# Gelu's table loaded by a one-column activation, small sine tables made after the first normalized tiles, table arguments kept in w2's tile, and a new order of work

## The chip, the cores and the metric

The kernel runs on one core of a Trainium2 chip. A core has a matrix engine (TensorE, PE in the profile; its weight loads are shown as PEld), a vector engine (VectorE, DVE), an activation engine (ScalarE, ACT), GpSimd (POOL), and SyncE (SP), which here only issues DMAs. Each engine works through its own instructions strictly in the order in which they were written and waits on semaphores for the others. The metric is the device time of one execution in microseconds (us), compared by the median over runs.

## The reference

`x` is `A_q` (2048 x 640, bf16). It is layer-normalized to `xn`, which feeds two branches:

```python
xn = _layernorm(x, axis=-1)
# A: four-tap causal shift convolution of k, times v, then a causal convolution over 2048 places
k_shift = sum over t of k_pad[:, t:t + S, :] * shift_k[:, ks - 1 - t]
kv = k_shift * v
y = irfft(rfft(kv padded to 2 S) * rfft(ssm_k padded))[:S] + kv * ssm_D
s = xn * y
# B: a two-layer MLP, 640 -> 1728 -> 640
g = silu(gelu(xn @ w1 + b1) @ w2 + b2)
return x + s * g
```

Here `gelu` is the tanh approximation.

## The kernel before, in words

Sequence rows are held as 16 tiles of 128 partitions x 640 columns. The kernel is a list of small named operations, each tied to one engine, and a string `ORDER` that names them in the order in which they are written out. This order is fixed by hand; each engine's queue is the sub-list of its own operations. `/A` and `/D` behind a name put an eviction from PSUM on ACT or on DVE. Where two operations share a buffer the framework adds the semaphore wait. Temporary buffers come from pools, handed out first-freed-first in the order of the string: three PSUM pairs `ps`, two PSUM banks `psf`, four staging buffers `st`, three gate buffers `sl`.

The names that matter:

- Loads on SP: `xl` (x), `Kl` (the long filter ssm_k, held for now in x and xn tiles 8 to 15; `Kl4` is the small piece with filter tiles 6 and 7), `w1l`, `w2l`, `kl` (k), `vl` (v). `b1l`, `skl` (the shift taps) and `Dl` are issued by ACT.
- Sine tables. `wq`, `wr` on DVE compute integer arguments (L223 to L229) in a scratch `Pq`, and `ws0`, `ws1`, `ws2` on ACT (L234) turn them into the first Fourier matrix W with Sin. The small tables F2 and I1 come from `sm0` (seven iotas on POOL, L242 to L247), `sm1` (nine small DVE instructions), `ss` (two Sin activations on ACT, L271 and L272) and `sx` (a scaling on POOL, L275).
- `warm` and `dm0`, `dm1`, `dm2`: matmuls on zeros, whose results nobody reads (L666, L673). `wm`/`we`: the shift taps broadcast to all partitions (PE L321, evicted by L176).
- Layer norm by tile: `bn` (DVE L382, L383), `rs` (POOL L395, L396), `xn` (DVE L401), `xt` (PE transposes L411), `xe` (eviction L176).
- MLP: `f1` (PE L431; `f1h`, L445, the last 64 columns of w1), `ge`/`geh` (Gelu, ACT L437, L451), `f2` (PE L467), `si` (Silu, ACT L471), `gx` (xn times gate, DVE L473). A name such as `f1_1_0_9` is: chunk of four tiles, part, column tile of w1. Column tiles 0-1, 2-4, 5-8 and 9-13 of w1 arrive with `w1l0` to `w1l3`.
- Convolution: `kv` (taps and product with v, DVE L495 to L504), stage 1 `K1`, `K1r` for the filter and `U1`, `U1r` for kv (PE L342, L357), evicted by `Ke`, `Ker`, `Ue`, `Uer` (L176) and written to scratch DRAM by `Ks`, `Us` (SP). They are read back transposed by `KL`, `UL`; stage 2 `K2`, `U2`, `X2` (PE L538, L552); products `pm`, `pq` (DVE L567); stage 3 `j1`, `j1r` (PE L573); `cs` and `cl` go through scratch DRAM once more; the last stage is `i2` (PE L640), then `ym` (times xn, DVE L644), `ad` (plus x, DVE L648, L656) and `os` (store). `Da` (POOL L303) adds ssm_D to the filter's first row.

The activation tables are loaded by an instruction that the compiler puts ahead of the first activation of a new set. If that activation waits for a matmul, so does the load.

Of the kernel before, what the change touches and what calls it, by code (L numbers as in the profile page):

```python
# [99 lines left out]
def h3_block(ctx: ExitStack, tc: tile.TileContext, x_d, k_d, v_d, sk_d, K_d, D_d, w1_d, b1_d, w2_d, out_d):  # L100
# [139 lines left out]
    def sm0(e):  # L240
        g = nc.gpsimd
        g.iota(pi, pattern=[[0, 1]], base=0, channel_multiplier=1)  # L242
        g.iota(k2s, pattern=[[0, 1]], base=0, channel_multiplier=1, allow_small_or_imprecise_dtypes=True)
# [1 line left out]
        g.iota(ng, pattern=[[0, 6], [1, 16], [16, 2]], base=0, channel_multiplier=0, allow_small_or_imprecise_dtypes=True)
# [446 lines left out]
ge_0_1_3 K1_10 K1_1 ge_0_1_2 ge_1_0_10 Ke_10/A f1_0_0_10 ge_0_0_10 f1_0_1_4 ge_0_0_11 ge_0_1_4 ge_0_1_5 Ke_1/A
f1_0_1_6 f1_0_2_12 ge_0_1_6 kv1_1a Da ge_0_1_7 K1r_0 rs4 vl1 w2l1 ge_0_2_12 K1_0 w2l0 xn15 f1_0_1_0 Ke_2/A ge_0_1_0
ge_0_1_1 f1_0_1_10 ge_0_1_11 kl2 ge_0_1_10 f1_0_0_8 kv1_2m kv1_2a ge_0_0_9 ge_0_0_8 f1_0_1_8 Ke_0/A ge_0_1_8 Ks_5
ge_0_1_9 xn12 kv1_3m kv1_3a Ker_0/A Ks_4 kv1_4 kv2_0 vl2 f2_7_1 kv2_1m Ks_0 kv2_1a kv2_2m si_7_1 gx_7_1 Ks_1 kv2_2a
kl3 kv2_3m ss f2_3_1 U1_2 Ue_2/A si_3_1 U1_3 U1r_0 Uer_0/A Ue_3/A f2_1_1 si_1_1 U1_1 gx_1_1 Us_1 f2_0_1 Ue_1/A kv2_3a
gx_3_1 kv2_4 kv3_1m kv3_0 si_0_1 vl3 U1_0 Ue_0/A Us_0 U1_7 U1r_1 Uer_1/A f2_6_0 U1_4 Ue_7/A U1_6 Ue_6/A si_6_0 f2_5_0
gx_0_1 kv3_1a gx_6_0 Ue_4/A kv3_2m kv3_2a si_5_0 gx_5_0 kv3_3m kv3_3a xn14 U1_8 U1_9 U1_5 kv3_4 f2_4_1 Us_3 Ue_5/A
Ue_9/A xt12 si_4_1 U1r_2 U1_10 kv4_0 gx_4_1 Ue_8/A xe12/A xl4 kv4_1m f2_5_1 KL1 f2_6_1 Uer_2/A U1_11 si_5_1 gx_5_1
kv4_1a kv4_2m bn8 KL2 kv4_2a Ue_10/A si_6_1 Ue_11/A U1_12 Us_4 U1_13 xt14 xe14/A Us_2 Ue_12/A Ue_13/A f2_2_1 kv4_3m  # L700
# [1 line left out]
xt15 Uer_3/A Ue_14/A f2_3_0 xe15/A K2_1 Ue_15/A Us_6 si_3_0 xn13 f2_0_0 Kf_1_0/A si_0_0 f2_4_0 si_4_0 Us_7 sx gx_3_0
KL0 rs3 xn9 gx_0_0 xn10 xt9 K2_3 xe9/D Kf_1_1/A xt10 f2_7_0 xn11 xn8 Kf_3_0/D xe10/A Kf_3_1/A xt13 si_7_0 K2_0 f2_1_0
gx_7_0 xe13/A Kf_0_1/A Kf_0_0/D gx_4_0 UL0 UL1 UL3 si_1_0 xt11 xe11/A X2_0 Xf_0/D U2_0 xt8 xe8/D gx_1_0 Uf_0_1/A
pq_0_0 f1_3_0_1 UL2 ge_3_0_1 UL5 Uf_0_0/D pq_0_1 UL4 U2_1 Uf_1_1/A f1_3_0_0 ge_3_0_0 Uf_1_0/D pm_1_0 pm_1_1 f1_2_0_4
ge_2_0_4 U2_3 X2_1 Uf_3_0/A Uf_3_1/A f1_2_0_7 ge_2_0_7 f1_3_0_11 pm_0_1 j1_1 Xf_1/A je_1_1/A f1_3_0_5 ge_3_0_11
je_1_0/D ge_3_0_5 X2_3 pm_0_0 U2_2 f1_2_0_11 Uf_2_1/A Uf_2_0/D gt f1_3_0_9 Xf_3/A j1_0 ge_2_0_11 f1_2_0_1 ge_3_0_9
je_0_1/A pq_1_0 pq_1_1 j1r_0 ge_2_0_1 pm_2_1 jer_0_1/A je_0_0/D KL4 UL7 jer_0_0/A f1_2_0_0 pm_2_0 X2_2 ge_2_0_0 K2_4
f1_3_0_4 Xf_2/D Kf_4_1/A pm_3_0 Kf_4_0/A ge_3_0_4 j1_2 f1_2_0_5 je_2_1/A je_2_0/D X2_4 U2_4 ge_2_0_5 f1_3_0_8 pm_3_1
f1h_2 KL5 Uf_4_0/D Xf_4/A j1_3 Uf_4_1/A cs_0 ge_3_0_8 geh_2 pq_2_1 pq_2_0 f1_2_0_10 je_3_0/A K2_5 pq_3_0 pm_4_1 cs_1  # L710
je_3_1/D ge_2_0_10 UL6 f1_2_0_6 Kf_5_1/A U2_6 KL6 Kf_5_0/D X2_5 pq_4_0 f1_3_0_7 Uf_6_0/D ge_2_0_6 Uf_6_1/A U2_5 Xf_5/A
Uf_5_0/A f1_3_0_10 pq_3_1 pm_4_0 j1_4 Uf_5_1/D ge_3_0_7 ge_3_0_10 pq_5_0 X2_6 f1_3_0_2 je_4_0/A je_4_1/D j1r_1 Xf_6/A
jer_1_1/A ge_3_0_2 KL7 pm_5_1 pm_5_0 jer_1_0/A f1_3_0_6 K2_7 Kf_7_1/A Kf_7_0/D f1_2_0_3 X2_7 pq_6_1 ge_3_0_6 Xf_7/D
cs_2 K2_6 Kf_6_0/A f1_2_0_12 j1_5 pq_5_1 pq_7_0 pq_6_0 Kf_6_1/D ge_2_0_3 ge_2_0_12 f1_2_0_2 je_5_0/A U2_7 ge_2_0_2
Uf_7_0/A cs_3 f1_3_0_12 f1_3_0_3 Uf_7_1/A ge_3_0_12 pq_7_1 pq_4_1 je_5_1/D pm_6_0 j1r_2 pm_6_1 f1_2_0_8 ge_3_0_3
jer_2_0/A ge_2_0_8 jer_2_1/D j1r_3 f1_2_0_9 jer_3_1/A j1_6 ge_2_0_9 cs_5 pm_7_0 f2_11_0 jer_3_0/D cs_4 pm_7_1 je_6_1/A
# [47 lines left out]
```

## Time and profile before

| | |
|---|---|
| median of 3 runs | 185.07 us (185.06 to 185.65) |
| profiled execution | 184.39 us, span 182.60 us |
| PE busy | 175.6 us, 96% of the span |
| DVE busy | 157.8 us, 86% |
| ACT busy | 143.9 us, 79% |
| POOL busy | 16.4 us, 9% |
| DMA | 50.32 MB, mean 276 GB/s |

The span runs from the first to the last instruction; the profiled execution's own time is 1.79 us longer. Busy times are the union of an engine's instructions. In a timeline row the columns are start, duration, engine, source line, operation, tiles and shapes, and in brackets the idle time before it with what ended it. Rows of neighbours that are alike are merged.

### The profile page before, as it was taken

How to read it: one execution, taken by the hardware profiler on the slowest of the kernel's cores; microseconds unless marked ns; L12 is line 12 of the kernel's file. 1: busy time of each engine (PE TensorE's matmuls, PEld its weight loads, DVE VectorE, ACT ScalarE, POOL GpSimd, SP SyncE). 2: the span in 40 equal slices, each digit the busy share in tenths (PEclk: the TensorE clock that was granted, in tenths of full speed). 3: DMA queues.
4: the chain of work that ended last, by engine and by line, in shares of the span. 5: the costliest groups of instructions: out<-in, count | busy, mean ns of one | idle time of the engine just before them, and what ended most of it. 6: DMA issues, size and time to landing. Idle time of an engine off the chain costs nothing.

```text
...
## 1 busy us (share of the span) xinstructions
PE 175.6 (96%) x2109; PEld 104.0 (57%) x2109; DVE 157.8 (86%) x258; ACT 143.9 (79%) x212; POOL 16.4 (9%) x32
## 2 busy tenths in 40 slices
...
GB/s 152 353 396 314 274 380 375 301 419 403 404 52 356 335 340 372 359 306 284 289 391 310 90 224 385 242 166 147 163 127 108 317 157 344 304 250 323 117 216 180
DMA packets 24503, 50.32 MB, mean 276 GB/s; under 512 B 3807, under 2 KB 18465, under 8 KB 24226
## 3 DMA queue, kind: packets, MB, share of 16 engines
...
HBM read 31.14 MB, written 18.35 MB: 271 GB/s over the span
## 4 chain that ended last, share of the span: by engine, by line
PE 72%; DVE 11%; ACT 11%; DMA 2%; issue 2%; SPq 0%; ACTq 0%
PE psf L431 27%; PE psf L467 25%; DVE xn L644 6%; PE ps L573 6%; PE ps L538 5%; ACT st L176 4%; PE ps L342 4%; ACT hT L437 3%; DVE x L648 3%; DMA x<-in_ssm_k 2%; PE psf L411 2%; DVE xn L473 1%; PE ps L552 1%; DVE x L656 1%; ACT ku L176 1%
## 5 line engine op out<-in xcount | busy, mean ns | idle before, releaser
L467 PE MATMUL psf<-w,hT 128*64 128x320 bf16 (+6 forms) x672 | 65.0, 299 | 0.0
L431 PE MATMUL psf<-xnT,w 128*128 128x512 bf16 (+1 forms) x320 | 61.9, 340 | 0.1
L467 PEld LDWEIGHTS <-hT 128*64 128x64 bf16 (+3 forms) x672 | 47.5, 106 | 14.8 <-issue 3.2
L431 PEld LDWEIGHTS <-w 128*128 128x128 bf16 x320 | 28.9, 98 | 27.8 <-issue 9.2
L176 ACT CAST ku<-ps 128x1024 bf16<-128x1024 f32 (+1 forms) x42 | 39.3, 961 | 2.4 <-PE ps L321 0.8
L176 ACT CAST st<-ps 128x1024 bf16<-128x1024 f32 x39 | 39.3, 1028 | 0.3 <-PE ps L342 0.2
L437 ACT ACTIVATE hT<-psf,b1f 128x512 bf16<-128x512 f32 (+1 forms) x64 | 36.9, 619 | 2.9 <-PE psf L431 2.5
L471 ACT ACTIVATE sl<-psf 128x320 bf16<-128x320 f32 (+2 forms) x32 | 14.3, 445 | 26.8 <-PE psf L467 21.2
L176 DVE CAST ku<-ps 128x1024 bf16<-128x1024 f32 (+1 forms) x25 | 28.7, 1153 | 4.8 <-PE ps L573 2.6
L567 DVE TENSOR_TENSOR st<-ku 128x512 bf16<-128x512 bf16 (+1 forms) x32 | 25.0, 815 | 0.6 <-PE ps L573 0.5
L473 DVE TENSOR_TENSOR xn<-xn,sl 128x320 bf16<-128x320 bf16 (+2 forms) x32 | 10.1, 322 | 11.7 <-ACT sl L471 11.7
L499 DVE TENSOR_TENSOR ku<-ku 128x2560 bf16<-128x2560 bf16 (+1 forms) x15 | 19.1, 1275 | 0.2
L502 DVE TENSOR_TENSOR ku<-ku 128x2560 bf16<-128x2560 bf16 (+1 forms) x15 | 18.2, 1214 | 0.2
L382 DVE BATCH_NORM_STATS2 stats<-x 128x6 f32<-128x320 bf16 x32 | 13.7, 469 | 0.2 <-DMA x<-in_x 0.2
L644 DVE TENSOR_TENSOR xn<-ps,xn 128x640 bf16<-128x640 f32 x16 | 12.5, 814 | 1.4 <-PE ps L640 1.4
L573 PE MATMUL ps<-st,I 32*64 32x512 bf16 (+1 forms) x384 | 11.2, 344 | 0.0
L538 PE MATMUL ps<-ku,F 64*32 64x512 bf16 x256 | 10.0, 380 | 0.0
L176 ACT COPY xnT<-psf 128x640 bf16<-128x640 bf16 x12 | 8.4, 724 | 0.0
L573 PEld LDWEIGHTS <-I 32*64 32x64 bf16 x384 | 4.8, 104 | 6.1 <-issue 3.8
L411 PE MATMUL psf<-ident,xn 128*128 128x128 bf16 x80 | 7.0, 220 | 1.0 <-ACT hT L437 0.7
L401 DVE TENSOR_SCALAR xn<-x,mv,rstd 128x640 bf16<-128x640 bf16 x16 | 7.5, 492 | 0.1
L411 PEld LDWEIGHTS <-xn 128*128 128x128 bf16 x80 | 5.1, 97 | 4.2 <-issue 2.8
...
## 6 DMA issues: line engine op xcount, KB each, us to landing
...
```

The costliest lines, as they stand in the source:

```text
L176: (nc.scalar.copy if e == "ACT" else nc.vector.tensor_copy)(out=out_, in_=in_)
L411: nc.tensor.transpose(out=o[:, t, :], in_=xn_t[:, i, t * P:(t + 1) * P], identity=ident[:])
L431: nc.tensor.matmul(out=pb.v[:, u * n:u * n + n], lhsT=w1_t[:, ft, t, :], rhs=xnTb[c].v[:, a // P:(a + n) // P, t, :], start=(t == 0), stop ...
L437: op("ge_%d_%d_%d" % (c, r, ft), "ACT", lambda e, c=c, ft=ft, u=u, a=a, n=n, pb=pb: nc.scalar.activation(out=hTb[c].v[:, ft, a:a + n], in_ ...
L467: nc.tensor.matmul(out=pb.v[m:n, 0:hw], lhsT=hTb[c].v[0:M, ft, q * P + m:q * P + n], rhs=w2_t[0:M, ft, hs], start=(ft == 0), stop=(ft == F ...
L471: op("si_%d_%d" % (i, h), "ACT", lambda e, pb=pb, s_=s_, hw=hw: nc.scalar.activation(out=s_.v[:, 0:hw], in_=pb.v[:, 0:hw], func=ACT.Silu), ...
L499: op("kv%d_%dm" % (r, j), "DVE", lambda e, i=i, n=n, j=j, t=t, wb=wb: nc.vector.tensor_tensor(out=t.v[:, 0:n, :], in0=k_t[:, i + 3 - j:i + ...
L502: op("kv%d_%da" % (r, j), "DVE", lambda e, n=n, t=t, a=a: nc.vector.tensor_tensor(out=a.v[:, 0:n, :], in0=a.v[:, 0:n, :], in1=t.v[:, 0:n, ...
L538: nc.tensor.matmul(out=pb[ri].v[32 * j:32 * j + 32, a, :], lhsT=F2_t[64 * a:64 * a + 64, ri, :], rhs=B.v[64 * a:64 * a + 64, j, 0:512], st ...
L567: nc.vector.tensor_tensor(out=o, in0=u, in1=k, op=ALU.mult)
L573: nc.tensor.matmul(out=pb[j // 2].v[64 * a:64 * a + 64, j % 2, 0:n], lhsT=I1_t[32 * j:32 * j + 32, t, :], rhs=rhs(slice(32 * j, 32 * j + 3 ...
L644: op("ym_%d" % i, "DVE", lambda e, i=i, pb=pb: nc.vector.tensor_tensor(out=xn_t[:, i, :], in0=pb.v.rearrange("p a b -> p (a b)")[:, 0:D], ...
```

## The change

Four edits:

1. A new operation `tg`: one Gelu activation of one column, from the constant `cst` into a new tile `tg` that nothing reads. It stands on ACT behind `ws0` and ahead of the first `ge`, and waits only for the constant, so the load of Gelu's table stands ahead of it and not ahead of the first `ge`.
2. `sm0` now reads the first two normalized tiles: it begins with a POOL copy of two elements of them, so its seven iotas come after `xn0` and `xn1`.
3. The scratch `Pq` lies in w2's tile and not in k's. So the load of w2's first piece waits for the `ws`, and the first two loads of k no longer do.
4. `IDLE` has 10, 2 and 4 matmuls in place of 10, 6 and 5, and `ORDER` is new. `Kl4` is issued ahead of `xl0` and `xl1`, `w1l2` ahead of `xl3`, `w1l3` ahead of `Kl2`, and both ahead of the first `Ks`; `xn1` is made ahead of `xn0`; `f1_1_0_9` is the second matmul group of its chunk (it was the eighth); `KL2` is ahead of `KL1`; `ss` is later; the last stage takes its tiles in another order. From `xt9` to `f2_10_0` the order on PE is the same.

```diff
+    tg = sb.tile([P, 1], F32, name="tg")
...
-    Pq = k_t.rearrange("p a d -> p (a d)")[:, 0:4096].bitcast(I32)
+    Pq = w2_t[:].rearrange("p a d -> p (a d)")[:, 0:4096].bitcast(I32)
...
     def sm0(e):
         g = nc.gpsimd
+        g.tensor_copy(out=sct[0:1, 88:90], in_=xn_t[0:1, 0:2, 0])
         g.iota(pi, pattern=[[0, 1]], base=0, channel_multiplier=1)
...
-    op("sm0", "POOL", sm0, writes=[smb])
...
+    op("tg", "ACT", lambda e: nc.scalar.activation(out=tg[:], in_=cst[:, 0:1], func=ACT.Gelu_apprx_tanh), reads=[cb])
...
-             writes=[kb[g]] + (Pqb if g < 2 else []))
+             writes=[kb[g]])
...
+    op("sm0", "POOL", sm0, reads=[xnb[0][0], xnb[1][0]], writes=[smb])
...
-        load("w2l%d" % g, "SP", [(w2_t[:, a:b, :], w2_d[:, a:b, :])] + rest, writes=[w2b[g]])
+        load("w2l%d" % g, "SP", [(w2_t[:, a:b, :], w2_d[:, a:b, :])] + rest, writes=[w2b[g]] + (Pqb if g == 0 else []))
...
-IDLE = ((10, 1), (6, 1), (5, 0))
+IDLE = ((10, 1), (2, 1), (4, 0))
 ORDER = """
-xl0 b1l grid xl1 zz warm skl Kl4 one0 id Dl fix c0 wq1 wq2 wr1 ws1 wr2 xl3 xl2 w1l0 bn0 ws2 K1_6 one1 b1c bn1 rs0 sm0
-wm2 wm0 dm0 wq0 we0/A w1l2 w1l1 wr0 Ke_6/A wm1 dm1 xn0 we1/A xt0 xn1 bn6 bn4 Kl1 xe0/A bn5 xt1 dm2 xe1/A bn7 f1_0_0_6
-we2/D ws0 rs2 f1_0_0_4 K1_7 Kl3 ge_0_0_6 ge_0_0_7 bn3 Ke_7/D bn2 kl0 ge_0_0_4 K1r_1 ge_0_0_5 xn4 K1_5 Ker_1/A f1_0_0_0
-f1_0_0_2 Ke_5/A ge_0_0_1 ge_0_0_0 xn7 ge_0_0_3 ge_0_0_2 xn5 K1_14 K1_4 Ks_3 Kl2 xt4 xt7 Ke_4/A w1l3 K1_12 xe4/D rs1
-xe7/A xn6 xn2 xt5 xe5/D kv0_1m kv0_0 xn3 kv0_1a kv0_2m sm1 Ke_12/A xt6 Ks_2 K1r_3 xt2 xl5 K1_15 xe6/A xe2/A kv0_2a
-bn12 bn14 f1_1_0_6 Ke_15/A ge_1_0_6 f1_1_0_1 ge_1_0_1 Ker_3/A f1_1_0_8 ge_1_0_8 f1_1_0_0 ge_1_0_0 K1_11 Ke_14/A f1h_1
...
+zz grid c0 Kl4 b1l Dl warm one0 id one1 fix wq1 xl0 wq2 wr1 wr2 skl xl1 bn0 bn1 b1c rs0 ws1 w1l2 K1_6 wm0 xl3 ws2 wq0
+we0/A wr0 xn1 xn0 bn6 Ke_6/A bn5 bn7 wm2 dm0 bn4 wm1 dm1 we1/A xt1 w1l0 xe1/A xt0 xl2 w1l1 Kl1 K1_7 dm2 xe0/A f1_0_0_6
+f1_0_0_4 ws0 tg ge_0_0_7 ge_0_0_6 we2/D ge_0_0_4 ge_0_0_5 sm0 K1_5 rs2 Ke_5/A K1r_1 Ker_1/A f1_0_0_0 f1_0_0_2 ge_0_0_1
+ge_0_0_0 bn2 bn3 rs1 Ke_7/D Kl3 ge_0_0_3 ge_0_0_2 kl0 xn4 xn7 xn5 K1_4 Ke_4/A K1_15 K1_12 xt4 xe4/D xt7 xe7/A xn6 xt5
+xn2 Ke_12/A xe5/D xt6 K1r_3 xt2 kv0_0 K1_14 w1l3 Kl2 xe6/A f1_1_0_0 xe2/A kv0_1m Ke_15/A f1_1_0_9 ge_1_0_0 ge_1_0_9
+Ker_3/A sm1 kv0_1a Ks_3 f1_1_0_6 f1_1_0_8 K1_8 xl5 Ks_2 ge_1_0_6 ge_1_0_8 f1h_1 f1_1_0_11 xn3 geh_1 kv0_2m Ke_14/A
+bn14 kv0_2a kv0_3m bn12 ge_1_0_11 Kl0 vl0 bn13 Ks_7 f1_1_0_1 ge_1_0_1 xt3 K1_13 kl1 K1_11 xe3/A f1_1_0_4 Ke_13/A Ks_6
...
-kv4_3a kv4_4 si_2_1 K2_2 KL3 gx_6_1 Us_5 bn9 f2_2_0 Kf_2_1/A U1_15 bn11 Kf_2_0/A bn10 gx_2_1 si_2_0 U1r_3 gx_2_0 U1_14
...
+U1_12 U1_13 kv4_2m si_5_1 gx_6_1 kv4_2a Us_2 gx_5_1 kv4_3m xl4 kv4_3a xt14 bn10 Ue_11/A f2_2_1 Ue_12/A xe14/A Us_4 KL1
+KL3 kv4_4 Ue_13/A K2_2 f2_2_0 Kf_2_0/A Kf_2_1/A bn8 si_2_1 U1_14 Us_5 U1r_3 U1_15 si_2_0 Uer_3/A f2_3_0 Us_6 Ue_15/A
...
-gx_9_1 i2_1 f2_8_0 ym_1 i2_9 i2_0 ad_11 ad_1 i2_8 geh_3 si_8_0 cl_6 cl_3 cl_7 ad_10 gx_8_0 ym_9 ym_0 ym_8 f2_13_1
-i2_13 i2_12 ym_13 ym_12 f2_12_1 i2_7 cl_2 si_13_1 os_11 ad_8 ad_0 gx_13_1 ym_7 si_12_1 i2_14 i2_6 f2_13_0 i2_5 ym_14
...
-f2_14_1 si_14_1 i2_2 ym_15 ym_2 ad_3 ad_2 os_2 os_12 os_3 f2_15_0 si_15_0 gx_14_1 ad_14_1 gx_15_0 ad_15_0 os_14
-os_15_0 f2_15_1 si_15_1 gx_15_1 ad_15_1 os_15_1
...
+i2_4 i2_5 ym_4 f2_8_0 ym_10 ym_5 cl_1 i2_1 ad_10 geh_3 si_8_0 ad_4 i2_0 cl_3 cl_4 f2_13_1 si_13_1 os_4 ym_1 i2_13 ym_0
+os_10 os_11 f2_12_1 i2_3 ad_1 si_12_1 ad_0 ym_13 ad_5 os_5 i2_2 cl_7 i2_12 gx_13_1 gx_8_0 f2_13_0 si_13_0 ym_3 ym_2
...
+i2_8 i2_15 f2_15_0 si_15_0 ad_14_0 ad_14_1 os_14 f2_15_1 ym_8 ad_8 os_8 si_15_1 os_6 os_9 ym_15 gx_15_0 ad_15_0
+gx_15_1 ad_15_1 os_15_0 os_15_1
```

More of the change, by code (lines that the diff above doesn't have):

```diff
@@ L264, in sm1 @@
         bit(fiq, fiq, 31, ALU.bitwise_and)
-    op("sm0", "POOL", sm0, writes=[smb])
-    op("sm1", "DVE", sm1, writes=[smb])
     def ssin(e):
@@ L272, in ssin @@
         nc.scalar.activation(out=I1_t[:].rearrange("p a b -> p (a b)"), in_=iq, func=ACT.Sin, scale=s32, bias=cst[:, 0:1])
-    op("ss", "ACT", ssin, reads=[smb, cb], writes=[Fb, Ib])
-    op("sx", "POOL", lambda e: nc.gpsimd.tensor_single_scalar(
-        out=I1_t[:], in_=I1_t[:], scalar=2.0 / 4096.0, op=ALU.mult), reads=[], writes=[Ib])
+    op("tg", "ACT", lambda e: nc.scalar.activation(out=tg[:], in_=cst[:, 0:1], func=ACT.Gelu_apprx_tanh), reads=[cb])
     for i in range(2):
@@ L455, in h3_block @@
         op("geh_%d" % c, "ACT", geh, reads=[pb, b1b], writes=[hTf[c][FT - 1]], hold=[hTb[c]])
+    op("sm0", "POOL", sm0, reads=[xnb[0][0], xnb[1][0]], writes=[smb])
+    op("sm1", "DVE", sm1, writes=[smb])
+    op("ss", "ACT", ssin, reads=[smb, cb], writes=[Fb, Ib])
+    op("sx", "POOL", lambda e: nc.gpsimd.tensor_single_scalar(
+        out=I1_t[:], in_=I1_t[:], scalar=2.0 / 4096.0, op=ALU.mult), reads=[], writes=[Ib])
     def f2_tile(i):
@@ L692 @@
[L692 to L700, printed above, removed]
-kv4_3a kv4_4 si_2_1 K2_2 KL3 gx_6_1 Us_5 bn9 f2_2_0 Kf_2_1/A U1_15 bn11 Kf_2_0/A bn10 gx_2_1 si_2_0 U1r_3 gx_2_0 U1_14
@@ L702 @@
[L702 to L716, printed above, removed]
@@ new lines @@
+ge_1_0_4 f1_1_0_7 f1_1_0_5 Ke_11/A kv0_3a ge_1_0_7 K1_9 Da ge_1_0_5 bn15 Ke_8/A f1_1_0_3 ge_1_0_3 f1_1_0_2 Ke_9/A
+ge_1_0_2 f1h_0 kv0_4 K1r_2 geh_0 K1_2 K1_3 Ker_2/A f1_1_0_12 f1_0_1_2 ge_1_0_12 f1_1_0_10 Ke_3/A K1_10 ge_0_1_3
+ge_0_1_2 ge_1_0_10 K1_1 Ke_10/A f1_0_0_10 ge_0_0_11 ge_0_0_10 f1_0_2_12 Ke_1/A f1_0_1_6 K1_0 ge_0_2_12 ge_0_1_7
+ge_0_1_6 kv1_1m kv1_0 K1r_0 rs4 kv1_1a xn15 f1_0_1_4 f1_0_0_8 Ke_2/A ge_0_1_4 ge_0_1_5 kl2 f1_0_1_8 ge_0_0_9 ge_0_0_8
+ge_0_1_8 vl1 f1_0_1_10 w2l1 kv1_2m kv1_2a ge_0_1_9 ge_0_1_10 ge_0_1_11 Ker_0/A w2l0 Ks_4 f1_0_1_0 Ks_5 ge_0_1_1 xn14
```

31 lines of the change are left out of this document (24 added, 7 removed).

## The prediction

> **What bounds the kernel now.** I read first the busy times and the span in 40 slices, then the engines by stage, then the timeline of the first 22 us, of 28 to 40 and of 74 to 80 us, then the DMA issues with their landings.
>
> ```profile
> PE 175.6 (96%) x2109; PEld 104.0 (57%) x2109; DVE 157.8 (86%) x258; ACT 143.9 (79%) x212; POOL 16.4 (9%) x32
> ...
> 0.00:6.00 6.00, 4.39 (x11) 1.54 (x12) 4.91 (x15) 3.31 (x5) 3.29 (x13) 1.00 0.68 201
> 6.00:13.90 7.90, 7.44 (x62) 4.87 (x63) 7.57 (x22) 6.62 (x9) 3.08 (x10) 1.00 0.98 372
> 13.90:21.80 7.90, 6.68 (x73) 4.43 (x70) 7.52 (x16) 7.89 (x16) 2.30 (x4) 1.00 0.89 307
> 21.80:157.00 135.20, 135.08 (x1649) 73.82 (x1649) 116.29 (x162) 118.34 (x172) 7.67 (x6) 1.00 0.80 282
> 157.00:179.20 22.20, 22.05 (x326) 19.31 (x320) 20.92 (x44) 7.38 (x14) 0.00 (x0) 1.00 0.66 232
> ```
>
> The rows give start:end, length, busy PE, PEld, DVE, ACT, POOL, granted clock, DMA share, GB/s. From 21.8 us to the last matmul at 179.15 PE is never idle for more than 0.1 us: 157.1 of 157.4 us. So the time is the moment at which PE becomes full, plus fixed matmul work, plus the last gate and store (3.4 us). A gain must come from before 21.8, where PE stands or computes zeros; a loss is any new wait of PE behind it.
>
> ```profile
> 5.49 0.09 PEld L342 LDWEIGHTS <-W 64*128 64x128 bf16 x1 [0.42 <-issue]
> 6.02 0.39 PE L342 MATMUL ps<-x,W 64*128 64x512 bf16 x2 [0.46 <-DMA x<-in_ssm_k]
> 7.20 1.01 ACT L176 CAST ku<-ps 128x1024 bf16<-128x1024 f32 x1 [0.79 <-PE ps L321]
> 8.07 1.69 DVE L401 TENSOR_SCALAR xn<-x,mv,rstd 128x640 bf16<-128x640 bf16 x2
> 8.32 1.26 POOL L245 IOTA G<- 128x192 f32 x1
> 9.97 1.29 ACT L176 COPY xnT<-psf 128x640 bf16<-128x640 bf16 x2
> 11.14 1.02 ACT L234 ACTIVATE W<-ku,cst 128x256 bf16<-128x256 int32 x2
> 12.44 0.99 PEld L431 LDWEIGHTS <-w 128*128 128x128 bf16 x10 [0.17 <-DMA w<-in_w]
> 12.64 1.28 ACT L437 ACT_TABLE_LOAD   x1 [0.48 <-PE psf L431]
> ...
> 31.32 1.38 POOL L303 TENSOR_TENSOR x<-x,Dr 1x640 bf16<-1x640 bf16 x1 [12.60 <-DMA x<-in_ssm_k]
> 31.74 2.32 DVE L499 TENSOR_TENSOR ku<-ku 128x2560 bf16<-128x2560 bf16 x1
> ...
> 54.00 1.28 ACT L471 ACT_TABLE_LOAD   x1
> 55.29 0.44 ACT L471 ACTIVATE sl<-psf 128x320 bf16<-128x320 f32 x1
> ...
> 77.92 0.82 DVE L504 TENSOR_TENSOR ku<-ku 128x1280 bf16<-128x1280 bf16 x1
> ```
>
> Up to 21.8 the chain of waits runs through ACT: it waits 0.79 for the broadcast taps, is then busy from 7.20 to 12.16 without a break, waits 0.48 for the first f1 and loads Gelu's table. Then it is full until xe6 releases the second chunk's f1 at 21.84. One of the two normalizations took 1306 ns and the other 463 (the line's own durations): the slow one ends at 9.76, 0.18 after the 1.26 us iota.
>
> **The change, part by part.**
>
> *Kl4 first.* K1_6 stood with its weights at 5.49 and waited for Kl4 until 6.02; its W is ready at 4.98 (two of the four Sin activations from 3.97). With Kl4 first in SP's queue it starts at about 5.5, behind the warm-up matmuls. wm0 now stands ahead of wm2: 5.5 + 0.32 + 0.55 = 6.4 for its end, which was 7.16. ACT is free at 6.40 (end of ws2), so we0 starts at 6.4 and not 7.20: **0.8 us**. The price is that xl0 and xl1 land behind 320 KB. They were issued at 0.73 and 1.18 and landed a median 2.3 us later; DVE wants them at 4.73 and 5.76, so more than 1 us is left. On ACT's queue Dl passes skl, 0.23 us of issue, wanted only at 5.8.
>
> *Small tables behind xn0, xn1.* Both normalizations take 0.46: they end at 8.91, not 9.76. DVE gains **0.85 us**, unless xl3, now behind w1l2 (640 KB), is late: it was in by 7.6, the same bytes as now were in by about 9.2, and it is wanted at 8.9, so the gain is between 0.55 and 0.85. ACT, 0.8 us earlier, needs xt1 for 9.17: 8.53 + 0.05 + 0.45 = 9.03; it comes in time. The POOL copy of two elements costs at most what the 128x14 cast took (0.33) and at least nothing; POOL is idle from 10.04 to 13.85. Behind sm0 on POOL stands rs2, which needs bn of tiles 4 to 7 (13.77, now 12.9): sm0 ends near 11.3. sm1 comes at 22, so that is hidden as well.
>
> *Table load.* ws0 ends at 12.16 - 0.8 = 11.36; the load then follows at once, as at 54.00 (the activation ahead ended at 53.98, the one behind began at 55.29). It ends at 12.65 instead of 13.92. tg itself: the Sin activations of 64 and 192 columns started 0.23 us apart; one column is between 0.1 and 0.34, I take 0.2. First Gelu at 12.85, against 13.94: 1.09 us. The second f1 group bounds this: its w1l1 landed at 12.44. As the same bytes lie ahead of it, I let it stay there: third Gelu at 13.75 instead of 14.66, **0.9 us**. The next ACT steps (0.36 a Gelu, 0.9 an eviction) are back to back as before, so xe6 ends 0.9 earlier and PE is full from about 20.95. Fewer dummy matmuls (5 of 0.12) save nothing: they filled waits.
>
> The Trainium skill, "ScalarE: Activation LUTs", section "What ACT_TABLE_LOAD costs", has 1283 ns for the load and another 1380 ns of drain for every switch. The load agrees (1.28); the drain is not in the row at 54.00. By the rule the load would start at 12.74 and the first Gelu at 14.2, 0.3 us later than before.
>
> *w1l3 and k earlier.* f1_1_0_9 is now PE's second group of the chunk, wanted at 20.95 + 1.08 = 22.0. w1l3 (720 KB, issued 18.25, 8.4 us to landing) came at 26.6. Now about 5,840 KB land up to and with it. Before, 5,120 KB had landed with kl0 at 19.4 (12.18 + 7.3) and 6,400 KB with Kl2 at 24.8 (16.90 + 7.9); in between, 5,840 come at 22.5. The queue no longer stands still for Kl4 at the start nor for the first Ks at 16.5, worth 0 to 1 us: landing between 21.5 and 22.5, a wait of 0 to 0.5 us; I take **0.2 lost**. kl0 no longer waits for ws0 (12.16), but kv0_0 wants it only at 19.4. w2l0's new wait for the ws (over by 12) is nothing beside its issue at 34.4; kl2 ahead of it adds 640 KB, some 1.7 us of 46.1, and f2 reads w2 at 50.6.
>
> *DVE up to 79 us.* DVE is full from 4.7 to 82 and its kv4_4 (77.92 + 0.82 = 78.74) frees the second U1 group behind f2_2_0, at 79.01: a slack of 0.27. Now PE is there at 78.0 to 78.1. DVE: -0.85 (above), +0.24 (gx_6_1 moved ahead of kv4_4), -0.19 (bn12's wait for xl5 at 29.70). bn14, now at 27.0, may wait for xl5: by landed bytes up to 1.2 us. Against it stands POOL's L303, which held kv0_3m for 0.84 (2.32 against 1.48); that add now comes near 30.5, when kv0_3m runs or bn12 follows, and bn6 lost nothing beside POOL's last iotas. Bounds: -1.6 to +0.4; I take -0.8, so kv4_4 is done at 77.9: just in time.
>
> *Middle and tail.* KL2 is issued about 4 us earlier, K2_2's short wait goes (0.1). From xt9 PE's order stands. In the tail PE and DVE are both full; DVE's instructions are the same (16 ym at 0.73, 12 ad at 0.40, the gates), first ym is again behind seven half tiles of f2. i2_12 waited 0.27 for a PSUM buffer right behind i2_13; now f2_12_1 stands between. **0.2** gained (0 to 0.27).
>
> *Sum.* 0.9 - 0.2 + 0.2 = 0.9 us. The profiled execution had 184.39 us (span 182.60 and 1.79 around it); it would be 183.5. It lies 0.68 under the median, so for the median 185.07 - 0.9 = **184.2 us**.
>
> **Rivals.**
>
> 1. *PE waits for w1l3* (slower). The matmul order is strict, so all of PE stands until w1l3 is in. For: the landings above lie close to the need, and 640 KB took 7.9 us on this queue. Against: it needs 1 us more than the old curve. The gain is gone if it lands at 22.9, and it is slower beyond 0.3% from 23.5 on. Half way between 22.5 and Kl2's old 24.8, at 23.7, it costs 1.7: 185.07 - 0.9 + 1.7 = 185.9 us.
> 2. *DVE gives it back* (no change). bn14's wait is 1.2, POOL holds kv0_3m as before: kv4_4 at 78.74 - 0.85 - 0.19 + 0.24 + 1.2 = 79.1, and PE waits there from 78.1 until then: 185.1 us. For: slack of 0.27. Against: it needs both.
> 3. *The early load gains nothing* (no change). If the load still starts no sooner than 12.64, because the activation ahead of it must empty first, the first Gelu comes at 12.64 + 1.28 + 0.2 = 14.1, 0.2 later than before: 185.2 us. Against: the row at 54.00. The drain that the Trainium skill's page (above) states would be such a mechanism.
>
> **How the numbers follow.** 0.3% is 0.56 us, about what a measurement of this kernel can tell from no change. My case: 0.60; its own range, from 0 to 1.09 at the start, w1l3's 0 to 0.5 and the tail's 0.27, is 183.7 to 184.5. Rival 1: 0.13. Rival 2, with smaller parts of it: 0.17. Rival 3: 0.03. Other waits of the new order in the middle, where the slack is tenths: 0.07, slower. Faster 0.60; the same 0.20 (rivals 2 and 3); slower 0.20 (rival 1 and the other waits). The range runs from 183.6 to 185.9, which leaves out about 0.05 below and 0.12 above.
>
> **What would show it.** K1_6 at 5.5, we0 at 6.4; two normalizations of 0.46; the table load within 0.05 of ws0's end and the first Gelu near 12.9; the second chunk's f1 at 21.0, with no more than 0.3 us idle ahead of its second group; no PE idle ahead of U1_14; last matmul near 178.2. Wrong if the row of f1's weight loads names in_w near 22, if stage-1 matmuls near 78 wait for L504, or if DVE, not PE, ends last in the tail.

## The result and the profile after

The changed kernel takes 183.82 us (median of 7 runs, 183.08 to 184.36) where the kernel before takes 185.06 beside it (184.32 to 185.65): a ratio of 0.9943, 95% interval 0.992 to 0.9966. So it is 0.6% faster by the ratio, and the medians lie 1.24 us apart. The profiled execution of the changed kernel had 183.84 us with a span of 182.1; that of the kernel before, shown above, had 184.39 with 182.60. So this pair of profiles shows only 0.55 of the 1.24 us; where the rest is took other executions to see.

First the busy times and then the engines by stage, as they were shown of the kernel before (columns as there).

```profile
PE 175.1 (96%) x2104; PEld 103.9 (57%) x2104; DVE 158.2 (87%) x260; ACT 142.7 (78%) x211; POOL 18.2 (10%) x33
```

```profile
0.00:6.00 6.00, 4.83 (x13) 1.51 (x13) 4.89 (x15) 3.31 (x5) 3.32 (x13) 1.00 0.61 172
6.00:13.90 7.90, 6.82 (x55) 4.31 (x55) 6.46 (x20) 7.32 (x12) 3.17 (x10) 1.00 1.01 391
13.90:21.80 7.90, 7.19 (x77) 4.74 (x75) 7.80 (x18) 7.83 (x14) 2.23 (x4) 1.00 1.03 407
21.80:157.00 135.20, 134.63 (x1651) 73.82 (x1650) 117.63 (x165) 116.75 (x170) 9.53 (x6) 1.00 0.79 277
157.00:179.20 22.20, 21.62 (x322) 19.56 (x316) 21.05 (x45) 7.47 (x14) 0.00 (x0) 1.00 0.71 243
```

PE is busier between 13.9 and 21.8 (7.19 for 6.68), but it now stands for 0.57 us in all somewhere behind 21.8, where before it stood for 0.12 (134.63 of 135.20, was 135.08). In the last row it ends 0.5 sooner. The timeline of the changed kernel says where (start, length, engine, line, operation, tiles; in brackets the idle time ahead and what ended it):

```profile
5.98 0.39 PE L342 MATMUL ps<-x,W 64*128 64x512 bf16 x2
...
8.21 0.80 DVE L401 TENSOR_SCALAR xn<-x,mv,rstd 128x640 bf16<-128x640 bf16 x2
10.15 0.89 DVE L382 BATCH_NORM_STATS2 stats<-x 128x6 f32<-128x320 bf16 x2 [1.14 <-DMA x<-in_x]
...
11.99 1.28 ACT L277 ACT_TABLE_LOAD   x1
13.29 0.20 ACT L277 ACTIVATE tg<-cst 128x1 f32<-128x1 f32 x1
13.40 1.36 ACT L437 ACTIVATE hT<-psf,b1f 128x256 bf16<-128x256 f32 x3
...
12.98 1.26 PE L431 MATMUL psf<-xnT,w 128*128 128x256 bf16 x10 [0.59 <-DMA w<-in_w]
...
29.74 0.44 PE L411 MATMUL psf<-ident,xn 128*128 128x128 bf16 x5 [0.51 <-ACT hT L437]
```

Each edit did its own work: the two normalizations take 0.80 us together and not 1.69, the table load begins at ws0's end with no drain between, and the first Gelu comes at 13.40 for 13.94. And each met a new wait: VectorE 1.14 us for xl3 at bn6, PE 0.59 for w1l1 at its second f1 group, PE 0.51 at xt3 for a buffer that ge_1_0_11 reads late. K1_6 is at 5.98, for 6.02.

The chain of waits of the changed kernel leads to w1l1 (start, length, what):

```profile
0.72 3.31 DMA b1r<-in_b
...
4.04 0.33 SPq L289
...
4.41 1.21 SPq L289
...
5.67 7.27 DMA w<-in_w
...
12.98 1.28 PE psf L431 x10
```

SP's queue stood until the small bias load on ScalarE's queue had landed (4.03, where it landed at 3.21 before), then issued w1l0, xl2 and at 5.67 w1l1, which was issued at 4.31 before. That the later issue makes the landing late is not shown: in a second profile of the changed kernel (`again`, below) w1l1 was issued at 5.39, and its group started at 12.28, ahead of the 12.45 before.

### The profile page after: what moved, and what is told of

It reads as the page before. It is cut to its first block, busy times and chain, and to the rows that moved or that the text cites. A ratio compares the mean times of both kernels' runs of the same rounds, so it can differ in the third digit from the quotient of the medians.

```text
span 182.1 us, 5024 instructions
## 1 busy us (share of the span) xinstructions
PE 175.1 (96%) x2104; PEld 103.9 (57%) x2104; DVE 158.2 (87%) x260; ACT 142.7 (78%) x211; POOL 18.2 (10%) x33
## 4 chain that ended last, share of the span: by engine, by line
PE 81%; ACT 9%; DMA 6%; issue 1%; SPq 1%; DVE 1%
PE psf L473 33%; PE psf L431 26%; PE ps L579 6%; PE ps L544 5%; ACT st L178 4%; DMA w<-in_w 4%; PE ps L342 3%; ACT hT L437 3%; PE ps L646 2%; PE psf L411 2%; DMA b1r<-in_b 2%; PE ps L558 1%; PE psf L445 1%; PE ps L357 1%; SPq L289 1%
## 5 line engine op out<-in xcount | busy, mean ns | idle before, releaser
L178 ACT CAST ku<-ps 128x1024 bf16<-128x1024 f32 (+1 forms) x41 | 38.0, 957 | 2.4 <-PE ps L544 0.7
L178 DVE CAST ku<-ps 128x1024 bf16<-128x1024 f32 (+1 forms) x26 | 29.7, 1158 | 1.9 <-PE ps L579 0.7
L178 ACT COPY xnT<-psf 128x640 bf16<-128x640 bf16 x11 | 7.6, 712 | 0.8 <-PE psf L411 0.8
L401 DVE TENSOR_SCALAR xn<-x,mv,rstd 128x640 bf16<-128x640 bf16 x16 | 6.5, 439 | 0.1
```

Of the source, the lines that this page charges most:

```text
L178: (nc.scalar.copy if e == "ACT" else nc.vector.tensor_copy)(out=out_, in_=in_)
```

## The experiments

Times are medians; each kernel stands beside runs of the kernel before on the same chip. The differences are small beside the scatter of single runs (the kernel before lies between 184.1 and 185.7 in nearly all), so I also followed each profile's PE by milestones, which repeat to some hundredths of a us.

**The new start, the new middle, the new tail, each alone; and the changed kernel once more.** In `head` the new code runs with the new order up to f1_1_0_12; `mid` and `tail` are the old code with one stretch of the new order.

```diff
 head: new code
+ order: new, from zz to f1_0_1_2 (behind f1_1_0_12); then the rest in the old order
 mid: old code
+ order: old up to f1_0_1_2, Da, new up to ge_2_0_10, then old
 tail: old code
+ order: old up to ge_2_0_10 (some 119 us); then new
 again: the changed kernel, nothing edited
```

> The new code with the new order up to f1_1_0_12 (some 40 us into the span), and the old order from there to the end. Theory 1 (the prediction: the gain is made in the first 22 us, by the one-column Gelu, the later small tables and the earlier kernel load): all of the 1.2 us that the change gained, so 183.6 to 184.2 where the kernel before takes 185.06. Theory 2 (the pair of profiled executions: what the start gains is lost by f1_1_0_2, and only the order behind 40 us keeps something, 0.25 us in the middle and 0.25 at the end): within 0.3 us of the kernel before, 184.8 to 185.3. Theory 3 (both hold a half): 184.3 to 184.7.

> The old code and the old order up to f1_1_0_12 and again from KL4 on (some 100 us); between them the new order (KL2's load earlier, the f2 and U1 stages interleaved anew, bn8 to bn11 behind it). Theory 1 (all at the start): within 0.3 us of the kernel before. Theory 2: 0.25 us or more faster (184.8 or less), and in the profile no wait of K2_2 for the load KL2. A third reading, that the new middle is only good behind the new start: slower than the kernel before by over 0.3.

> The old code and the old order up to some 110 us, and the new order from there to the end (what differs is behind jer_2_0: cl loads, i2 and f2 tiles of the last 22 us). Theory 1: within 0.3 us of the kernel before. Theory 2: 0.25 us faster (184.8), the 0.27 us that i2_12 waited for a bank of PSUM gone from the profile.

> The changed kernel once more, for a second profile and for its time beside the three parts on one chip: 183.8, 0.5 to 0.7% under the kernel before. If head, mid and tail each do their part alone, their three gains sum to this one's within 0.4 us; if not, a part needs another. In the profile: if the clock's step to full speed comes at another moment than 5.96 us from the span's start, then K1_6 and the first gelu move with it (theory: 0.43 us per warm-up matmul against 0.22); if the step is at 5.96 again, the moment belongs to the kernel and not to the run.

Measured, beside 184.73 us for the kernel before: head 184.58 (ratio 0.9989, 0.9969 to 1.0009), mid 184.74 (0.9998, 0.9977 to 1.002), tail 184.24 (0.9982, 0.9963 to 1.0001), again 183.64 (0.9939, 0.9916 to 0.9962). The times alone decide little: each part is within the scatter, only the whole is not. The three gains (0.15, -0.01 and 0.49 us) sum to 0.63 where `again` gained 1.09: 0.46 apart, for the 0.4 us allowed; but each ratio is known to some 0.37 us either way only, so this does not show that a part needs another. The profiles decide more. Starts of PE's groups in us, and the length of each stretch:

| profile | K1_6 | f1_1_0_12 | f2_3_0 | f1_2_0_9 | f2_15, second half | f1_1_0_12 to f2_3_0 | f1_2_0_9 to f2_15 |
|---|---|---|---|---|---|---|---|
| before | 6.02 | 38.00 | 80.06 | 139.97 | 177.61 | 42.06 | 37.64 |
| mid | 5.97 | 38.65 | 80.43 | 140.37 | 178.01 | 41.78 | 37.64 |
| tail | 5.90 | 38.10 | 80.14 | 140.05 | 177.42 | 42.04 | 37.37 |
| after | 5.98 | 38.01 | 79.79 | 139.72 | 177.09 | 41.78 | 37.37 |
| again | 5.29 | 37.30 | 79.08 | 139.02 | 176.38 | 41.78 | 37.36 |
| head | 5.35 | 37.34 | 79.38 | 139.29 | 176.93 | 42.04 | 37.64 |

The middle (0.26 to 0.28 us) and the tail (0.27) are the same wherever they stand, and add up. That is theory 2 for these two stages, by the profiles; the time of mid shows nothing of it. The start is neither theory: it varies from run to run, 37.30 to 38.01 with the new start and 38.00 to 38.65 with the old one. The rows show three things that vary.

One is the clock at the start. PE's timeline of `again`, the warm-up and K1_6:

```profile
1.17 4.18 PE L672 MATMUL psf<-hT 128*128 128x512 bf16 x11 [1.17 <-DVE cst L202]
5.29 0.39 PE L342 MATMUL ps<-x,W 64*128 64x512 bf16 x2
```

and the warm-up in the first profile of the changed kernel:

```profile
1.17 4.87 PE L672 MATMUL psf<-hT 128*128 128x512 bf16 x11 [1.17 <-DVE cst L202]
```

The same 11 matmuls take 4.18 us in one execution and 4.87 in another, since their pitch falls from 0.43 to 0.22 us at a moment that differs: behind the eighth in `again`, behind none of them in the first profile (the granted clock reads 1.00 throughout, so it is the pitch that tells). K1_6 stands behind the warm-up and follows it, and so does the first Gelu (13.40 and 12.71). With the old start an early step gains little, as Kl4 lands at 5.57 to 5.97; K1_6 starts at 5.90 to 6.02 in every profile. But only in the first profile of the kernel before is it Kl4 that K1_6 waits for: in mid and tail the step was late, and the warm-up itself ended at 6.04 and 5.97. So a part of the gain at K1_6 between these profiles is the luck of the step. The Trainium skill, "TensorE: Matmul & The Clock Gate", section "What's actually happening", has the window that decides as free-running, so that the moment differs from run to run, and counts 6, 11 or 14 slow matmuls in runs of one kernel. The variation agrees: 8 slow ones in `again`, 11 in the first profile.

The second is w1l1, on which the second f1 group (f1_0_0_4) waits in five of the six profiles below. `again` is 0.70 ahead of the first profile at every milestone to the end, and it looks as if K1_6 carried that. It doesn't by itself, as two more runs with the new start show (notg and warm9, described further down). Starts on PE in us:

| profile | K1_6 | f1_0_0_4 (its wait for w1l1) | f1_1_0_0 | f1_1_0_12 |
|---|---|---|---|---|
| after | 5.98 | 12.98 (0.59) | 21.48 | 38.01 |
| again | 5.29 | 12.28 (0.58) | 20.76 | 37.30 |
| head | 5.35 | 12.32 (0.56) | 20.81 | 37.34 |
| notg | 5.40 | 13.02 (1.21) | 21.51 | 38.03 |
| warm9 | 5.03 | 12.68 (1.03) | 21.17 | 37.70 |
| headmid | 5.91 | 12.16 (0.00) | 21.22 | 37.75 |

In the five profiles in which f1_0_0_4 waits, f1_1_0_12 comes 25.0 us behind it, wherever K1_6 stood: in notg K1_6 is 0.58 ahead of the first profile, and f1_1_0_12 is level with it. So w1l1's landing sets the new start there. In `again` and `head` it came early together with K1_6; in notg and warm9 it did not. The loads ahead of it in the queue move with it (w1l2 lands at 8.58 in the first profile, 7.76 in `again`, 8.58 in notg); why they come earlier or later is not shown, and w1l1 further forward in the queue was not tried.

The third is w1l3. PE's timeline of `mid` and, behind it, of `tail`, which both have the old start:

```profile
27.33 0.74 PE L445 MATMUL psf<-xnT,w 128*64 128x256 bf16 x10 [0.73 <-DMA w<-in_w]
```

```profile
26.78 0.74 PE L445 MATMUL psf<-xnT,w 128*64 128x256 bf16 x10 [0.25 <-DMA w<-in_w]
```

and the weight load in the first profile of the kernel before:

```profile
26.67 0.47 PEld L445 LDWEIGHTS <-w 128*64 128x64 bf16 x10 [0.33 <-DMA w<-in_w]
```

f1h_1 waits for w1l3 by 0.73, 0.25 and 0.03 us: in the first profile it landed just as PE came. From K1_6 to f1_1_0_12 the old start takes 31.95 us in all three if that wait is left out; the new one 32.03, 32.01 and 31.99 in after, again and head (31.84 in headmid, 32.63 in notg and 32.67 in warm9, by w1l1's landing), with no such wait (w1l3 lands at 18.9 to 20.9, and is wanted at 21.8 or later).

**Single pieces put into the kernel before, and the changed kernel with the old tail.**

```diff
 kl4
-xl0 b1l grid xl1 zz warm skl Kl4 one0
+Kl4 xl0 b1l grid xl1 zz warm skl one0
 w1l3
-bn2 kl0 ge_0_0_4 ... Ke_4/A w1l3 K1_12
+bn2 kl0 w1l3 ge_0_0_4 ... Ke_4/A K1_12
 tg
+op("tg", "ACT", lambda e: nc.scalar.activation(out=tg[:], in_=cst[:, 0:1], func=ACT.Gelu_apprx_tanh), reads=[cb])
-ws0 rs2
+ws0 tg rs2
 headmid: new code
+ order: new up to ge_2_0_10; then old
```

> The kernel before with one thing moved: Kl4, the load that K1_6 reads, is issued first on SP's queue, ahead of xl0. Theory A (the start's gain is K1_6, which now waits for the warm-up matmuls and so for the moment at which the clock steps up, and no longer for Kl4's landing at 5.6 to 6.0): K1_6 starts at 5.3 to 6.0 us by the run, and the time falls by 0.1 to 0.7 us, unless w1l3's landing (26.6 to 27.3 in three profiles of this start) takes it back at f1h_1: then under 0.2 us, and the profile shows f1h_1 waiting for w1l3 by as much as K1_6 gained. Theory B (the start's gain is the early table load and the small tables): no change within 0.2 us, K1_6 and all behind it where they were.

> The kernel before with one thing moved: the load w1l3 is issued right behind kl0 (some 12.5 us in) and not behind Ks_3 and Kl2 (18.3 us). Theory A (the kernel before loses at f1h_1 in most of its runs, 0.03, 0.73 and 0.25 us in three profiles, as w1l3 lands at the moment at which PE asks for it, and the change's earlier w1l3 ends that): 0.2 to 0.4 us faster in the median, f1h_1 with no wait. Theory B (those waits are chance, made up for later): within 0.15 us.

> The kernel before with one operation more: the one-column Gelu right behind ws0 on ScalarE. Both theories: the table load moves to 12.2 to 13.5 us, the first gelu from 13.94 to some 13.5. Theory A (ScalarE's gain at the first gelu doesn't reach the end, as PE waits next for w1l3 and later for others): within 0.2 us of the kernel before. Theory B (the prediction: the first gelu carries the start): 0.4 us faster.

> The new code and the new order up to some 110 us, the old order behind it: the changed kernel with the old tail. If each stage keeps its gain to the end (theory A): 0.25 us slower than the changed kernel, so 183.9 to 184.1 where the kernel before takes 184.7; f1_2_0_9 at 139.0 to 139.8 by K1_6's moment (5.3 to 6.0), i2_12 waiting 0.27 us again. If the new start needs the new middle to keep its gain (the new start with the old middle came out at 184.6 only), then this one is 0.5 us or more faster than that. If the tail is what makes the difference (theory C): 184.4 to 184.7.

Measured, beside 184.66 us for the kernel before: kl4 184.80 (1.0004, 0.9987 to 1.0021), w1l3 184.45 (0.9985, 0.9968 to 1.0002), tg 184.48 (0.9983, 0.9964 to 1.0001), headmid 184.29 (0.998, 0.9961 to 1.0).

kl4 gained nothing, but not for the reason that I had written down. PE's timeline of it:

```profile
11.75 1.49 PE L431 MATMUL psf<-xnT,w 128*128 128x256 bf16 x11 [0.29 <-DMA w<-in_w]
```

With Kl4 in front, every load behind it is later, and w1l2, which the first f1 group reads, lands at 11.71 (11.19 before): the group starts at 11.75 for 11.30. The warm-up was also long in this execution (K1_6 at 5.98). With a step that late Kl4 could have gained nothing at K1_6 in this execution. That Kl4 first needs the other part of the new load order, w1l2 fourth in SP's queue, to be worth anything is argued from these rows, not shown. tg alone moved the first Gelus (the first in time from 13.94 to 13.68) and the second chunk's first f1 group (15.6 us behind K1_6, for 15.8 in before, mid and tail), and then f1h_1 waited for w1l3:

```profile
27.40 0.74 PE L447 MATMUL psf<-xnT,w 128*64 128x256 bf16 x10 [1.03 <-DMA w<-in_w]
```

which is theory A. In w1l3 the wait is gone and f1_1_0_12 stands at 37.96, 0.04 ahead of the kernel before, whose own wait had been small in the profile; the time is 0.2 us lower, at the edge of what was expected, and the interval still holds no change. headmid's profile has the middle at 41.78 and the tail at 37.64, as they should be, and its start between the others (K1_6 5.91, f1_1_0_12 37.75). But its time, as that of `head`, is some 0.5 us above what the stretches sum to (184.66 - 0.65 - 0.26 = 183.75; measured 184.29), and in the range of none of the theories. One more load with no room shows in it:

```profile
120.74 0.63 PE L544 MATMUL ps<-ku,F 64*32 64x512 bf16 x16 [0.24 <-DMA ku<-scrU]
```

U2_6 waits for UL6, which is late or less than 0.55 us ahead of its need in eight of the fourteen profiles, with the old order and the new. Whether that is what their longer executions lose is not shown: the profile of `head` is its shortest execution (183.70 of 183.70 to 185.47).

**Parts undone in the changed kernel, and two attempts to go further.**

```diff
 notg
-op("tg", ...)
-ws0 tg ge_0_0_7
+ws0 ge_0_0_7
 smearly
-g.tensor_copy(out=sct[0:1, 88:90], in_=xn_t[0:1, 0:2, 0])
-rs0 ws1 ... ge_0_0_5 sm0 K1_5
+rs0 sm0 ws1 ... ge_0_0_5 K1_5
 warm9
-NWARM = 11
+NWARM = 9
 best: NWARM = 9, and
-ws1 w1l2 K1_6 wm0 xl3 ... geh_1 kv0_2m Ke_14/A bn14 kv0_2a kv0_3m bn12 ge_1_0_11
+ws1 xl3 w1l2 K1_6 wm0 ... geh_1 kv0_2m ge_1_0_11 Ke_14/A bn14 kv0_2a kv0_3m bn12
```

> The changed kernel without the one-column Gelu. The table load then begins behind the wait for f1_0_0_6, 0.4 us later than now (12.39 for 12.00 in the profile of the changed kernel), the first gelu at 13.78 for 13.40. Theory A (in the changed kernel ScalarE is busy without a gap from the first gelu to beyond 22 us, and xt3 waits for it at 29 us, so its delay stays): 0.3 to 0.4 us slower than the changed kernel, some 184.0 to 184.1 where that takes 183.7. Theory B (the early load is covered by other waits): within 0.15 us of 183.7.

> The changed kernel with the small tables (sm0) on GpSimd where they were, ahead of the first normalized tiles. xn1 or xn0 takes 1.3 us again for 0.45, so xe0, ws0 and the first gelu come 0.6 to 0.9 us later. Theory A (ScalarE's chain carries it): 0.5 to 0.9 us slower than the changed kernel, 184.2 to 184.6. Theory B (VectorE waits for xl3 at bn6 anyway, 0.5 to 1.1 us in the profiles, and PE for xt3, so it is covered): within 0.2 us.

> The changed kernel with 9 warm-up matmuls for 11. Theory (K1_6 waits for the warm-up, whose length hangs on the moment at which the clock steps up): K1_6 starts at 5.0 to 5.2 in every run, at half or full speed, we0 at 6.3 to 6.5 in every run for 6.3 or 6.9; so the median falls by some 0.3 us (183.4), and what falls away are the longer times. If the clock steps up later because there was less to warm it, or K1_6 waits for its table ws1 (done at 4.85): no gain.

> The changed kernel with 9 warm-up matmuls, with ge_1_0_11 ahead of Ke_14's eviction on ScalarE, and with xl3's load ahead of w1l2's. Expected in the profile: xt3 no longer waits (0.51 us before), of which 0.3 stay, since ScalarE has no gap there and f1_1_0_4 waits next; bn6 no longer waits for xl3; f1_0_0_6 may wait for w1l2 by 0 to 0.3. So 0.3 to 0.6 us under the changed kernel, 183.1 to 183.4. If xt3's wait was ScalarE's load and not its order: as warm9.

Measured, beside 184.93 us for the kernel before: notg 183.69 (0.9938, 0.9916 to 0.996), smearly 183.96 (0.9961, 0.9942 to 0.9981), warm9 183.89 (0.9964, 0.9933 to 0.9996), best 183.52 (0.9953, 0.9918 to 0.9989).

notg gives up the early table load and loses nothing that can be measured: its ratio is that of the changed kernel (0.9943 and 0.9939). ScalarE's and PE's timelines of it:

```profile
11.90 1.28 ACT L435 ACT_TABLE_LOAD   x1 [0.49 <-PE psf L429]
...
13.02 1.26 PE L429 MATMUL psf<-xnT,w 128*128 128x256 bf16 x10 [1.21 <-DMA w<-in_w]
```

The load waits 0.49 us for the first f1 again, as foreseen, but PE's second f1 group waits for w1l1 until 13.02 anyway. That is theory B; w1l1 was late by more in this execution than in the others with this start and 11 warm-up matmuls (waits of 0 to 0.59), so the rows explain this one run and the median carries the verdict. smearly's profile ends where that of the changed kernel ends: K1_6 at 5.98 in both, f1_1_0_12 at 38.02 and 38.01. Its slow normalization is there, and covered:

```profile
8.07 1.69 DVE L399 TENSOR_SCALAR xn<-x,mv,rstd 128x640 bf16<-128x640 bf16 x2
9.99 0.89 DVE L380 BATCH_NORM_STATS2 stats<-x 128x6 f32<-128x320 bf16 x2 [0.24 <-DMA x<-in_x]
```

VectorE comes to bn6 0.75 us later than in the changed kernel, and xl3 is only then there. By the ratios 0.3 to 0.4 us remain (0.9961 beside 0.9943 and 0.9939), with intervals that overlap: between the two theories, while the profile speaks for B.

In warm9 K1_6 starts at 5.03, and it waits there for its table ws1, not for the warm-up:

```profile
1.17 3.50 PE L672 MATMUL psf<-hT 128*128 128x512 bf16 x9 [1.17 <-DVE cst L202]
5.03 0.39 PE L342 MATMUL ps<-x,W 64*128 64x512 bf16 x2 [0.36 <-ACT W L236]
```

That lead is gone at the second f1 group, which waits for w1l1:

```profile
12.68 1.26 PE L431 MATMUL psf<-xnT,w 128*128 128x256 bf16 x10 [1.03 <-DMA w<-in_w]
```

and U2_6 loses 0.47 us more to UL6, so this execution (184.09 us) gained nothing on those of the changed kernel. The times fall into two groups: 8 executions between 182.99 and 184.09, and 4 between 185.31 and 185.41. best has 7 between 182.95 and 183.60 and 5 between 185.04 and 185.26. No kernel with 11 warm-up matmuls shows such a second group, only single long executions (185.97 in mid, 188.88 in tail). So the expectation for the median was wrong: the long executions did not fall away, they became longer, and lie some 1.8 us above the others. No profile fell on one of them. The same page of the Trainium skill, "TensorE: Matmul & The Clock Gate", section "What's actually happening", has the full clock after some 3.4 us of sustained work. If PE's pauses now spoil one such stretch (it stands 0.36 us ahead of K1_6), half speed goes on for another 3.4 us, which as an estimate from that page costs 1.7. That fits the gap, and is only argued. In best's profile xt3 no longer waits, and f1_1_0_4 waits 0.20 for ScalarE in its place:

```profile
28.43 0.44 PE L411 MATMUL psf<-ident,xn 128*128 128x128 bf16 x5
...
29.76 3.40 PE L431 MATMUL psf<-xnT,w 128*128 128x512 bf16 x15 [0.20 <-ACT hT L437]
```

From the second f1 group to f1_1_0_12 best takes 24.75 us (12.35 to 37.10), the changed kernel 25.0: of the 0.51 us 0.27 are kept, about as expected, and bn6 no longer waits either. The median missed its range (183.1 to 183.4) as five of twelve executions lose some 1.8 us, and the intervals of best and the changed kernel overlap; the swap on ScalarE and xl3's place with 11 warm-up matmuls were not tried.

## Why the prediction came out as it did

The time of 184.2 was 0.4 above the 183.82 measured, the gain 0.9 for 1.24, and the sign right. But the terms are not those of the sum. From the profiles with old and new stretches the gain is: start 0.65 (mean of f1_1_0_12: 38.25 in before, mid and tail, 37.60 in after, again, head and headmid), middle 0.26, tail 0.27; 1.18 in all. The means of the start rest on three and four executions, which lie up to 0.71 apart.

For the start the sum had 0.9 - 0.2 = 0.7, and that this agrees with 0.65 is luck, as errors cancelled. Up to the second chunk's first f1 group the gain is 0.72 (mean 21.07, was 21.79; the sum had 0.9). Behind it 0.51 is lost at xt3, which the sum does not have. 0.34 is gained as f1h_1 no longer waits for w1l3, where the sum had 0.2 lost. 0.10 comes from other steps.

*Kl4 first* (K1_6 at 5.5, we0 at 6.4: 0.8 gained). Right mechanism, size wrong. The step that failed is "it starts at about 5.5, behind the warm-up matmuls", read off one execution as if the warm-up's end were fixed. It lies at 5.36 to 6.05; K1_6 came at 5.29, 5.35, 5.91 and 5.98, a mean gain of 0.33 at K1_6. What it was taken to release fails too: PE waits for w1l1 at the second f1 group, and in notg and warm9 an early K1_6 (5.40 and 5.03) brought f1_1_0_12 to 38.03 and 37.70 only. How much of the 0.33 reaches the end is open.

*Small tables behind xn0 and xn1* (0.55 to 0.85 for VectorE). The normalizations took 0.80 for 1.69, as said. The step that failed is xl3 "in by about 9.2", with the gain at 0.55 or more: it landed at 9.1 to 10.2, and VectorE gave back 0.25 to 1.28 us at bn6. Undone, it made no difference in the profile, and by the ratios 0.3 to 0.4 us with intervals that overlap.

*Table load* (first Gelu at 12.85, 0.9 kept). No drain, as read from the row at 54.00: at 11.99 the load follows ws0 at once, so rival 3 fell; the 1380 ns of drain in the Trainium skill, "ScalarE: Activation LUTs", section "What ACT_TABLE_LOAD costs", are not in this row. The first Gelu came at 13.40, in `again` at 12.71. The step after it, "xe6 ends 0.9 earlier and PE is full from about 20.95", came out in the mean only: PE came to the second chunk between 20.76 and 21.48, as w1l1 did not stay at 12.44 (its group started at 12.16 to 12.98). What failed is "full": PE paid 0.51 at xt3, as ScalarE's order has Ke_14 between geh_1 and ge_1_0_11, and I had not walked the two psf buffers through that part. From K1_6 to the second chunk's first group the new start takes 15.30 to 15.51 us for 15.83, and the 0.51 takes back what the table load and the small tables gained there: from K1_6 to f1_1_0_12 old and new both take about 32 us. The run without tg took no longer (183.69).

*w1l3* (0.2 lost; rival 1: 1.7 lost). The sign failed. It landed at 18.9 to 20.2, not 21.5 to 22.5, so PE does not wait. And it already cost something before: 0.03, 0.73 and 0.25 us at f1h_1 in three profiles of the old start, 1.03 with tg. The row was there to be read: the weight load of f1h_1 at 26.67, with w<-in_w as what released it, 0.01 us ahead of PE. I took its 26.6 as a landing and did not ask who wanted it then.

*DVE up to 79 us* (just in time; rival 2 else). kv4_4 was done at 78.54 in the first profile of the changed kernel, not 77.9, but PE came to U1_14 at 79.03 and did not wait; rival 2 did not happen. POOL's add went on holding a kv instruction (2.57 us beside 1.49 for its kind), and that stayed covered.

*Middle and tail* (0.1 named for the middle but left out of the sum, 0.2 for the tail). The tail is right: 0.27 in every profile. i2_13 and i2_12 stood back to back in the kernel before (PE's timeline):

```profile
162.63 1.01 PE L640 MATMUL ps<-ku,G 128*64 128x512 bf16 x8
163.44 2.10 PE L467 MATMUL psf<-w,hT 128*64 128x320 bf16 x28
```

and stand apart in the changed one:

```profile
162.37 0.46 PE L646 MATMUL ps<-ku,G 128*64 128x512 bf16 x4
162.65 2.09 PE L473 MATMUL psf<-w,hT 128*64 128x320 bf16 x28
```

A pair took 0.81 us to the next group's start; one takes 0.28 now, and the other as much elsewhere. The middle's 0.26 has another source than the 0.1 for K2_2's wait. In the kernel before:

```profile
58.17 0.39 PE L342 MATMUL ps<-ku,W 64*128 64x512 bf16 x2
58.49 2.08 PE L467 MATMUL psf<-w,hT 128*128 128x320 bf16 x14
60.50 0.61 PE L342 MATMUL ps<-ku,W 64*128 64x512 bf16 x4
```

and in `again`:

```profile
57.48 0.60 PE L342 MATMUL ps<-ku,W 64*128 64x512 bf16 x4
58.02 2.08 PE L473 MATMUL psf<-w,hT 128*128 128x320 bf16 x14
```

A U1 group followed by another U1 group takes 0.22 to 0.23 us to the next start, followed by f2 0.31 to 0.32 (two of them here: 0.54; one: 0.32); an f2 half tile takes 1.92 followed by f2 or a transpose and 2.01 followed by U1. So each change between the 64-row and the 128-row forms costs 0.09. From f1_1_0_12 to f2_3_0 the old order has 22 such changes, the new one 20: 0.18 us. In the first profile of the kernel before another 0.07 is f2_2_1's step to K2_2 (2.07, now 2.00), the wait that the prediction named. head and tail, with the old middle, have 2.00 there too and still take 0.26 more than the new one; what their last 0.08 is stays open, as no other step differs by more than 0.03. PE is never idle there by the profile, which is why I saw nothing to gain. The Trainium skill, "TensorEngine Tiling (Array Packing)", section "Key Properties", says that a change of tiling mode drains TensorE; it has no figure, the rows give 0.09 us; that a drain is what takes it is not shown.

As to the width: the range held the time. The chance for faster (0.6) rested on the table load and Kl4, which gave 0.72 up to 21 us and kept 0.2 of it behind xt3; w1l3, the main ground for the chance of slower, was a gain. Two figures do not follow from their terms: with nothing gained at the start and 0.5 lost on w1l3 the main case would reach 185.6, not 184.5; and rival 1 counts w1l3's 0.2 twice (185.07 - 1.1 + 1.7 = 185.7, not 185.9). The profiled execution of the kernel before lay 0.68 below its median, which I noted and did not follow up: it was one with almost no wait for w1l3.

What stays open: what moves w1l1's landing, why `head` and `headmid` came out some 0.5 us above the sum of their stretches, and what the long executions of warm9 and best lose.
